# A newly laid order for the first eight pairs of an attention and feed-forward kernel, with third buffers and other load queues

## The chip, the cores and the metric

The kernel runs on one core of a Trainium2 chip. The metric is the device time of one execution in microseconds (us); smaller is better. The time before is 367.57 us, the median of 3 runs (366.59 to 367.79).

## The reference, cut to what matters

```python
q, k, v: (8, 8, 576, 64) float32; bias_table: (32, 8); w_in: (512, 2048); w_out: (2048, 512)

scores = q @ k.T / sqrt(64) + bias_table[bucket(|i - j|)]     # by batch and head
attn = softmax(scores)
x = (attn @ v) with batch and position as 4608 rows, heads side by side as 512 columns
h = x @ w_in
out = max(0.01 * h, h) @ w_out                                # (4608, 512) float32
```

The bias depends on the distance |i - j| alone, and from a distance of 128 on it is one constant for each head.

## The kernel before, in words

**Work items.** A pair is two heads of one batch; there are 32 pairs, four to a batch (`n_pairs` is 4), numbered 0 to 31. For each pair the kernel makes the transposed scores, the exponentials, the product with V and a division, and puts the result, transposed, into `xT`. Once the four pairs of a batch are in `xT`, the feed-forward of the finished tokens may run: blocks `T` of 512 tokens, each with 16 input pieces (four matmuls of 512 columns each, then the leaky relu into `gt`) and 16 output parts (four matmuls each; four parts make a 128-row slice of the output).

**A pair's steps, with their lines.** `load_qk` (L114) brings q and k with POOL's DMA queue, turned into bf16 on the way. `turned_pair` (L277 and L281) transposes them on TensorE into a bank of the pool `ps_m` (tag "m", two banks). `transpose_q` (L296) copies q to `qt`, `transpose_k` (L303) copies k to `kt`, and `apart` (L288) makes the two heads' last 64 keys stand apart. `qk_mm(n, u)` makes one of six groups of scores: u = 0 to 3 are 128 keys by 512 queries for both heads (L331, two matmuls on half of the rows each), u = 4 the last 64 queries (L324), u = 5 the last 64 keys (L334, L335). Groups 0 to 3 and 5 go to the pool `ps_s` (two buffers), group 4 goes to the two banks of `ps_o` (tags "o0" and "o1"). `exp(n, u)` is ScalarE's exponential into the pair's buffers `at` and `at4` (L344, L351, L355). `band(n, u)` (L371, VectorE) multiplies the part near the diagonal by the bias factors `hk`; groups 0, 1, 2, 4 and 5 have such a part. `av_tails` (L384) and `av` (L395) multiply by V into the banks "o0" and "o1", one for each head, and `divide` (L404, L406) normalizes into `opair`. `x_transposes` (L451, L452) turns that through a bank "m" and copies it into `xT`; for pairs 6 to 30, except 7, a DMA does it (L441).

**The bias factors.** The table is loaded on SP's queue (L155), turned by one exponential (L168), and spread over a row `ub` of 512 numbers for each head by copies (L171, L182, L185); of the eleven copies at L182 ScalarE has three and VectorE eight. The row is written to memory (`u_row`, L191) and read back on SP's queue as `hk` and `hk4` in seven loads (L193, L200): heads 0 and 1, then 2 and 3, then 4 to 7.

**The order.** Nothing is rescheduled: every engine runs its instructions in the order in which the program calls them, and each waits for what it needs. For pairs 0 to 4 the order is written out by hand with calls such as `score(n, u)`, which is `qk_mm` and `exp`. From pair 5 on a loop with a small planner (`plan`, `slot`, `moe_block`) places feed-forward pieces between the pairs' steps; from pair 8 on it uses bodies that run two products on the two halves of TensorE's rows (`body_in_halves` L639, `av_phase` L428, `body_in_lanes` L743). Until pair 8 it places 16 input pieces and 4 output parts. `spin` (L941) is TensorE work without use, which keeps its clock up.

**Buffers.** `qt`, `kt`, `at` and `at4` have two buffers each, pair n using number n % 2. `gt` has two buffers of 16 x 512.

**Loads.** POOL's queue issues them in program order: q and k of pair 0, of pairs 1 and 2, V of the first heads, and so on; at pair 0's `begin`, `load_w_in(0)` (half of `w_in`), V of batch 1 in four chunks, its tails, q and k of its heads 4 to 7, the second half of `w_in` and the first half of `w_out`; at pair 2 q and k of batch 2 and the second half of `w_out`.

Of the kernel before, what the change touches and what calls it, by code (L numbers as in the profile page):

```python
# [37 lines left out]
def kernel(  # L38
# [32 lines left out]
    qt_pool = ctx.enter_context(tc.tile_pool(name="qt", bufs=2))  # L71
# [10 lines left out]

    ident = per.tile([P, P], BF16, name="ident")
# [18 lines left out]
    own = per.tile([P, 2, SL], BF16, name="own")  # L102
    ATW = 2 * NJ * S
    at_ = [per.tile([P, ATW + SL], BF16, name=f"at{i}") for i in range(2)]
    at4_ = [per.tile([P, S + SL], BF16, name=f"at4_{i}") for i in range(2)]

# [42 lines left out]
    clear_edges(nc.vector, 0)  # L149
    nc.vector.memset(own, 0.0)  # L150
# [5 lines left out]
    load_qk(0, 0, 2)  # L156
# [16 lines left out]
    for u, lo, hi in bucket_runs(NB, BAND, S):  # L173
        if lo >= small:
            w = hi - lo + 1
            if groups and groups[-1][2] == w:
                groups[-1][3] += 1
            else:
                groups.append([u, lo, w, 1])
    for j, (u, lo, w, m) in enumerate(groups):  # L180
        copy = nc.scalar.copy if j % 3 == 2 else nc.vector.tensor_copy
        copy(out=ub[:, C0 + lo : C0 + lo + m * w].rearrange("h (m w) -> h m w", w=w),  # L182
             in_=e8[:, u : u + m].unsqueeze(2).to_broadcast([H, m, w]))
# [108 lines left out]

    def transpose_q(n):
        qt = qts[n] = qt_pool.tile([P, S], BF16, name="qt")
        copy = nc.scalar.copy if n <= n_pairs and n != 1 else nc.vector.tensor_copy
        copy(out=qt[:, 0:S].rearrange("p (r c) -> p r c", c=NC), in_=turned_pair(n, 0))  # L296

    def transpose_k(n):
        kt = kts[n] = kts_[n % 2]
# [10 lines left out]
    def qk_mm(n, u, swapped=False):  # L310

        qt, kt = qts[n], kts[n]
        if u == NJ:
            if in_lanes(n):
                t = ps_s_pool.tile([P, 2, 512], FP32, name="ps_s")
                ps = [t[:, e, :] for e in range(2)]
            elif swapped:
# [8 lines left out]
            return t if in_lanes(n) else ps  # L326
# [10 lines left out]

    def at_view(n):
        return at_[n % 2][:, 0:ATW].rearrange("p (e c i) -> p e c i", e=2, c=NJ)

    def exp(n, u, ps):
        at, at4 = at_view(n), at4_[n % 2]
        if u < NJ:
            nc.scalar.activation(at[:, :, u, 0:512], ps, AF.Exp, scale=scale)  # L344
        elif u == NJ and in_lanes(n):
# [8 lines left out]
        else:  # L354
            nc.scalar.activation(at4[:, 0:S], ps.rearrange("p e i -> p (e i)")[:, 0:S], AF.Exp, scale=scale)  # L355

    def band(n, u):
        b, p = items[n]
        at, at4 = at_view(n), at4_[n % 2]
# [5 lines left out]
        elif u == NJ:  # L365
            o, m = at[:, :, 3, 2 * P : S], mirrored(hp, 0, S - 2 * P)
        elif u == NJ + 1:
            o, m = at4[:, 3 * P : S], mirrored(hk4[:, p, :], 0, P + SL)
# [6 lines left out]
    def av_tails(n):  # L375

        b, p = items[n]
        at4 = at4_[n % 2]
        ops_[n] = op_pool.tile([P, NJ + 1, 2 * D], BF16, name="opair")
        ps = outs[n] = [ps_o_pool.tile([P, 512], FP32, name="ps_o", tag=f"o{e}") for e in range(2)]  # L380
        for ic in range(NJ + 1):
# [5 lines left out]

    def av(n, e):
        b, p = items[n]
        at = at_[n % 2]  # L390
        ps = outs[n][e][:, 0 : (NJ + 1) * (D + 1)].rearrange("p (i d) -> p i d", d=D + 1)
        for ic in range(NJ + 1):
            for c in range(NJ):
                o = (e * NJ + c) * S + ic * P
                nc.tensor.matmul(ps[:, ic, :], lhsT=at[:, o : o + P], rhs=vn[b % NBUF][:, c, 2 * p + e, :],  # L395
                                 start=False, stop=(ic == NJ and c == NJ - 1))
        divide(n, (e,))

    def divide(n, heads):
        opair = ops_[n]  # L400
        of = [outs[n][e][:, 0 : (NJ + 1) * (D + 1)].rearrange("p (i d) -> p i d", d=D + 1) for e in heads]
        rcps = [rc_pool.tile([P, NJ + 1, 1], FP32, name="rcp") for _ in heads]
        for ps, rcp in zip(of, rcps):
            nc.vector.reciprocal(rcp, ps[:, :, D : D + 1])  # L404
        for e, ps, rcp in zip(heads, of, rcps):
            nc.vector.tensor_tensor(out=opair[:, :, e * D : (e + 1) * D], in0=ps[:, :, 0:D],  # L406
                                    in1=rcp.to_broadcast([P, NJ + 1, D]), op=ALU.mult)
# [9 lines left out]
    def av_phase(n, phase, last=None):  # L417

        b, p = items[n]
        at = at_[n % 2]  # L420
# [14 lines left out]

    def x_transposes(n, spare=None):
# [13 lines left out]
        for ic in range(NJ + 1):  # L450
            nc.tensor.transpose(ps[:, ic * P : (ic + 1) * P], in_=opair[:, ic, :], identity=ident)  # L451
        nc.vector.tensor_copy(out=xT[p][:, b * S : (b + 1) * S], in_=ps[:, 0:S])  # L452

# [13 lines left out]

    def ffn_in(T, f, spare=None):
        if f == 0:
            gts[T] = gt_pool.tile([P, n_fc, TT], BF16, name="gt")  # L470
        t0 = T * TT
# [4 lines left out]
        for c in range(n_cc):  # L476
            nc.tensor.matmul(pm, lhsT=w_in_sb[:, c, f * P : (f + 1) * P], rhs=xT[c][:, t0 : t0 + TT],  # L477
                             start=(c == 0), stop=(c == n_cc - 1))
# [86 lines left out]
    def choose():  # L565
# [4 lines left out]
        return "in" if left("in") == 0 or left("in") * share >= left("out") * n_fc else "out"  # L570

# [408 lines left out]
    def spread_loads(n, part):  # L980
# [3 lines left out]
        nc.gpsimd.tensor_copy(out=tick, in_=at4_[n % 2][0:1, S - 1 : S] if part == 2 else  # L984
# [30 lines left out]
    spin(9)  # L1015
    transpose_q(0)
    transpose_k(0)
    spin(2)
    score(0, 0)
    score(0, 1)  # L1020
    begin(0)
    score(0, 2)
    score(0, 3)
    transpose_q(1)
    transpose_k(1)
    spin(2)
    score(0, 5)
    score(0, 4)
    transpose_k(2)
    score(1, 0)  # L1030
    score(1, 1)
    score(1, 4)

    begin(1)
    for u in (0, 1, 2, 5, 4):
        band(0, u)
    spin(3, ps_m_pool, "m")
    score(1, 2)
    spin(3, ps_m_pool, "m")
    score(1, 3)  # L1040
    transpose_q(2)
    band(1, 0)
    band(1, 1)
    av_tails(0)
    av(0, 0)
    score(1, 5)
    av(0, 1)
    score(2, 0)
    score(2, 1)
    x_transposes(0)  # L1050
    band(1, 2)

    begin(2)
    band(1, 5)
    band(1, 4)
    transpose_k(3)
    score(2, 2)
    score(2, 3)
    av_tails(1)
    av(1, 0)  # L1060
    band(2, 0)
    transpose_q(3)
    score(2, 5)
    av(1, 1)
    band(2, 1)
    score(3, 0)
    x_transposes(1)
    band(2, 2)
    score(2, 4)
    score(3, 1)  # L1070

    for n in range(3, n_pairs):
        begin(n)
        band(n - 1, 5)
        band(n - 1, 4)
        transpose_k(n + 1)
        score(n, 2)
        av_tails(n - 1)
        av(n - 1, 0)
        band(n, 0)  # L1080
        score(n, 3)
        av(n - 1, 1)
        transpose_q(n + 1)
        score(n, 5)
        band(n, 1)
        x_transposes(n - 1)
        band(n, 2)
        score(n, 4)
        score(n + 1, 0)
        score(n + 1, 1)  # L1090

    n = n_pairs
    begin(n)
    band(n - 1, 5)
    band(n - 1, 4)
    av_tails(n - 1)
    av(n - 1, 0)
    score(n, 2)
    av(n - 1, 1)
    score(n, 3)  # L1100
    transpose_k(n + 1)
    x_transposes(n - 1)
    finished(n - 1)
    band(n, 0)
    band(n, 1)
    score(n, 5)
    room["left"] = 4
    moe(1)
    band(n, 2)
    transpose_q(n + 1)  # L1110
    score(n, 4)
    moe(2)
    band(n, 5)
    band(n, 4)
    pair_rows(n + 2)
    moe(1)

    for n in range(n_pairs + 1, N + 1):
# [121 lines left out]
```

## Time and profile before

| what | value |
|---|---|
| median of 3 runs | 367.57 us |
| the profiled execution's own time | 366.07 us |
| its span, first to last instruction | 364.3 us |
| busy: TensorE, weight loads, VectorE, ScalarE, POOL | 355.5, 205.7, 190.6, 243.8, 98.3 us |
| granted TensorE clock, mean | 0.999 |
| HBM read and written | 37.68 and 9.45 MB |

Times in the profile count from the span's start. In a timeline row stand the start, the duration, the engine, the line, the operation, what is written and read, the count of merged instructions, and in brackets how long the engine had been idle before and what ended that. In the chain of waits each piece is what the end of the program hung on at that time. A busy TensorE is not TensorE at its peak, because matmuls overlap and their ends are modelled.

### The profile page before, as it was taken

The numbers are of one execution on the slowest core, as the hardware profiler recorded it, in microseconds if no ns is written. First come the engines' busy times: TensorE is split into PE (matmuls) and PEld (weight loads), VectorE is DVE, ScalarE is ACT, GpSimd is POOL, SyncE is SP. The second block draws the span as 40 slices with busy tenths as digits, with TensorE's granted clock in tenths as the row PEclk, the third lists the DMA queues.
The fourth block names the chain that finished last, engine by engine and source line by source line (L and its number), as shares of the span: only waits on it lengthen the run. The fifth ranks groups of instructions, "written<-read, shape, count | busy, mean of one in ns | idle before, by whom it ended". The sixth has DMA issues, their size and how long they took to land.

```text
span 364.3 us, 11901 instructions
## 1 busy us (share of the span) xinstructions
PE 355.5 (98%) x5081; PEld 205.7 (56%) x5101; DVE 190.6 (52%) x499; ACT 243.8 (67%) x364; POOL 98.3 (27%) x190
## 2 busy tenths in 40 slices
PE   7999999999999999999999999999999999999996
PEld 2565565555557776666666666656666544444443
DVE  3797887677755767555656665555554300200000
ACT  5998887479948888777777777777776274054111
POOL 8854422042334334423243334211000000000000
PEclk9999999999999999999999999999999999999999
DMA  8999999999898898998898989965113000200212
GB/s 100 196 196 175 207 205 140 154 166 112 99 138 128 104 155 126 140 130 125 119 126 127 115 123 129 122 107 98 49 50 49 31 29 0 88 29 0 86 60 86
DMA packets 104651, 40.26 MB, mean 111 GB/s; under 512 B 83472, under 2 KB 99096, under 8 KB 104600
## 3 DMA queue, kind: packets, MB, share of 16 engines
q0 software_dynamic: 53984, 18.36, 49.6%
q1 hardware_dynamic: 49320, 19.06, 27.1%
q10 hardware_dynamic: 1296, 2.10, 1.6%
q8 instruction: 40, 0.66, 0.8%
q14 instruction: 11, 0.09, 0.1%
HBM read 37.68 MB, written 9.45 MB: 129 GB/s over the span
## 4 chain that ended last, share of the span: by engine, by line
PE 90%; DMA 4%; DVE 2%; SPq 1%; ACT 1%; issue 1%; ACTq 0%; DVEq 0%
PE pm L743 35%; PE pm L477 16%; PE pm L518 16%; PE ps_o L428 7%; PE ps_s L331 7%; DMA hk<-u_row 3%; PE ps_o L395 3%; PE pm L639 1%; PE ps_o L384 1%; PE ps_s L743 1%; DMA u_row<-ub 1%; PE ps_tx L451 1%; PE pm L511 1%; SPq L200 1%; PE ps_s L324 1%
## 5 line engine op out<-in xcount | busy, mean ns | idle before, releaser
L344 ACT ACTIVATE at<-ps_s 128x1024 bf16<-128x1024 f32 x128 | 126.1, 1023 | 31.6 <-PE ps_s L331 31.6
L743 PE MATMUL pm<-xT,w_in_sb 64*128 64x512 bf16 x608 | 139.6, 376 | 0.0
L743 PE MATMUL pm<-w_out_sb,gt 64*128 64x512 bf16 x544 | 129.6, 376 | 0.0
L490 ACT ACTIVATE gt<-pm 128x512 bf16<-128x512 f32 x140 | 82.5, 602 | 41.9 <-PE pm L477 36.2
L371 DVE TENSOR_TENSOR at<-at,hk 128x768 bf16<-128x768 bf16 (+3 forms) x160 | 69.0, 451 | 31.4 <-ACT at L355 20.4
L743 PEld LDWEIGHTS <-w_in_sb 64*128 64x128 bf16 x608 | 51.8, 94 | 24.7 <-issue 1.2
L477 PE MATMUL pm<-xT,w_in_sb 128*128 128x512 bf16 x257 | 60.7, 379 | 0.7
L743 PEld LDWEIGHTS <-gt 64*128 64x128 bf16 x544 | 48.3, 94 | 22.1 <-issue 0.7
L518 PE MATMUL pm<-w_out_sb,gt 128*128 128x512 bf16 x260 | 58.9, 379 | 0.8 <-issue 0.5
L331 PE MATMUL ps_s<-qt,kt 64*128 64x512 bf16 x256 | 46.5, 378 | 1.7 <-ACT at L344 1.2
L518 PEld LDWEIGHTS <-gt 128*128 128x128 bf16 x268 | 25.6, 98 | 29.9
L477 PEld LDWEIGHTS <-w_in_sb 128*128 128x128 bf16 x268 | 25.2, 98 | 28.6
L121 POOL DMA_DIRECT2D vn<-in_v_dram x32 | 33.7, 1054 | 20.4 <-PE pm L743 5.2
L428 PEld LDWEIGHTS <-at 64*128 64x128 bf16 x1760 | 33.1, 94 | 3.8 <-issue 0.5
L428 PE MATMUL ps_o<-vn,at 64*128 64x65 bf16 x1760 | 35.2, 190 | 0.0
L355 ACT ACTIVATE at<-ps_s 128x576 bf16<-128x576 f32 x32 | 21.0, 657 | 18.4 <-PE pm L743 18.1
L984 POOL COPY tick<-opair 1x1 bf16<-1x1 bf16 x46 | 8.3, 181 | 81.9 <-DVE opair L406 81.6
L406 DVE TENSOR_TENSOR opair<-ps_o,rcp 128x320 bf16<-128x320 f32 x64 | 29.4, 488 | 1.5
L794 DVE COPY y<-pm 128x512 f32<-128x512 f32 x17 | 11.8, 692 | 27.6 <-PE pm L743 27.6
L531 DVE COPY y<-pm 128x512 f32<-128x512 f32 x11 | 7.6, 691 | 33.6 <-PE pm L518 30.8
L984 POOL COPY tick<-at 1x1 bf16<-1x1 bf16 x23 | 4.9, 213 | 62.3 <-DVE at L371 62.3
L331 PEld LDWEIGHTS <-kt 64*128 64x128 bf16 x256 | 13.7, 94 | 13.5 <-issue 6.6
(76 smaller groups left out, 321.9 us busy)
## 6 DMA issues: line engine op xcount, KB each, us to landing
out_dram<-y SPq DMA_DIRECT2D x28, 256.0 KB, 3.1
vn<-in_v_dram POOLq DMA_DIRECT2D x28, 128.0 KB, 4.5
qn<-in_q_dram POOLq DMA_DIRECT2D x22, 144.0 KB, 4.1
kn<-in_k_dram POOLq DMA_DIRECT2D x22, 144.0 KB, 3.3
w_in_sb<-in_moe_w_in_dram POOLq DMA_DIRECT2D x2, 1024.0 KB, 12.2
w_out_sb<-in_moe_w_out_dram POOLq DMA_DIRECT2D x2, 1024.0 KB, 17.4
out_dram<-y ACTq DMA_DIRECT2D x7, 256.0 KB, 2.0
qn<-in_q_dram POOLq DMA_DIRECT2D x5, 288.0 KB, 10.3
```

The lines of the kernel that those rows point to most:

```text
L121: nc.gpsimd.dma_start(out=vn[b % NBUF][:, c, h0:h1, 0:D], in_=v[b, h0:h1, c * P : (c + 1) * P, :].rearrange("h s d -> s h d"),)
L331: nc.tensor.matmul(ps[:, e, :], lhsT=kt[r, u * P : (u + 1) * P], rhs=qt[r, 0:512], start=True, stop=True)
L344: nc.scalar.activation(at[:, :, u, 0:512], ps, AF.Exp, scale=scale)
L355: nc.scalar.activation(at4[:, 0:S], ps.rearrange("p e i -> p (e i)")[:, 0:S], AF.Exp, scale=scale)
L371: nc.vector.tensor_tensor(out=o, in0=o, in1=m, op=ALU.mult)
L406: nc.vector.tensor_tensor(out=opair[:, :, e * D : (e + 1) * D], in0=ps[:, :, 0:D], in1=rcp.to_broadcast([P, NJ + 1, D]), op=ALU.mult)
L428: m = nc.tensor.matmul(outs[n][e][:, ic * (D + 1) : (ic + 1) * (D + 1)], lhsT=at[halves[r], o : o + P], rhs=vn[b % NBUF][halves[r], c, 2 * ...
L477: nc.tensor.matmul(pm, lhsT=w_in_sb[:, c, f * P : (f + 1) * P], rhs=xT[c][:, t0 : t0 + TT], start=(c == 0), stop=(c == n_cc - 1))
L490: nc.scalar.activation(g, pm, AF.Prelu, bias=0.0, scale=1.0, alpha=0.01)
L518: nc.tensor.matmul(pm, lhsT=gt[:, f, ts * P : (ts + 1) * P], rhs=w_out_sb[:, f, :], start=(f == 0), stop=(f == n_fc - 1))
L743: m = nc.tensor.matmul(o, lhsT=w, rhs=x, start=was is None, stop=need[bank] == 0)
L984: nc.gpsimd.tensor_copy(out=tick, in_=at4_[n % 2][0:1, S - 1 : S] if part == 2 else ops_[n - 2 + part][0:1, 0, 0:1])
```

## The change

1. The first pair's q is loaded as float32 on ScalarE's queue, as the program's first instruction, and ScalarE casts it into `qn`, after the exponential of the table. POOL's first load is k alone.
2. All eleven copies of the bias row are VectorE's.
3. `qt`, `kt`, `at` and `at4` get a third buffer, cut out of one of the two `gt` tiles, which isn't needed before block 1. Pairs 0 to 5 use number n % 3, later ones n % 2.
4. Pairs 0 to 7 run in an order that is a list of tokens, in place of the code by hand and of three turns of the loop. In it matmuls and exponentials, transposes and their copies, and the divisions are single steps; the product with V goes by chunks of 128 keys (`ac n e c`, all query blocks of a chunk); group 4's scores can take a `ps_s` buffer (`m n 4 s`, then one exponential for both heads); two input pieces of the feed-forward are begun on three of their four steps before pair 3 is there (`p0`, ended by `p1`); input pieces and their leaky relu are apart (`i`, `l`), with banks of `ps_m`, `ps_s` or `ps_o`. It holds the same 16 input pieces and 4 output parts. The q copies of pairs 5 and 7 move from VectorE to ScalarE.
5. `w_in` comes in quarters, V of batch 1 by single heads first, q and k of its heads 4 to 7 in two loads each.

The diff, cut to its core (`at_[n % 2]` becomes `at_[home(n)]` and likewise throughout; `blocks(n)` and `width(n)` are the old constants):

```diff
+    first_q = per.tile([96, 2, S // 96, D], FP32, name="first_q")
+    nc.scalar.dma_start(out=first_q.rearrange("r h c d -> r h (c d)"),
+                        in_=q[0, 0:2, :, :].rearrange("h (r c) d -> r h (c d)", c=S // 96))
...
+    early = gt_pool.tile([P, n_fc, TT], BF16, name="gt").rearrange("p f t -> p (f t)")
+    ATE = ATW + SL
+    at_.append(early[:, 0:ATE])
+    at4_.append(early[:, ATE : ATE + S + SL])
+    kts_.append(early[:, ATE + S + SL : ATE + 2 * S + SL + P])
+    qts_ = [per.tile([P, S], BF16, name=f"qt{i}") for i in range(2)]
+    qts_.append(early[:, ATE + 2 * S + SL + P : ATE + 3 * S + SL + P])
+
+    def home(n):
+        return n % 3 if n <= n_pairs + 1 else n % 2
...
+    clear_edges(nc.vector, 2)
...
-    load_qk(0, 0, 2)
+    load_qk(0, 0, 2, ("k",))
...
+    nc.scalar.copy(out=qn[0][0:RQ, 0:2, :, :], in_=first_q)
     for j, (u, lo, w, m) in enumerate(groups):
-        copy = nc.scalar.copy if j % 3 == 2 else nc.vector.tensor_copy
+        copy = nc.vector.tensor_copy
...
-    def load_w_in(half):
-        o = slice(half * (DF // 2), (half + 1) * (DF // 2))
+    def load_w_in(quarter):
+        o = slice(quarter * (DF // 4), (quarter + 1) * (DF // 4))
...
+    def av_chunks(n, e, chunks):
+
+        b, p = items[n]
+        at = at_[home(n)]
+        for c in chunks:
+            for ic in range(blocks(n)):
+                o = (e * NJ + c) * S + ic * P
+                nc.tensor.matmul(outs[n][e][:, ic * (D + 1) : (ic + 1) * (D + 1)], lhsT=at[:, o : o + P],
+                                 rhs=vn[b % NBUF][:, c, 2 * p + e, :],
+                                 start=False, stop=(ic == blocks(n) - 1 and c == NJ - 1))
...
+    def first_part():
+        T, f = step("in")
+        if f == 0:
+            gts[T] = gt_pool.tile([P, n_fc, TT], BF16, name="gt")
+        pm = bank("pm1")
+        in_steps(pm, T, f, range(n_cc - 1))
+        return pm, T, f
+
+    def last_part(pm, T, f, by_vector=0):
+        in_steps(pm, T, f, (n_cc - 1,))
+        leaky(T, f, pm, by_vector)
+        room["left"] -= 1
...
         if n == 0:
             load_w_in(0)
-            load_v_part(1, range(NJ))
+            load_w_in(1)
+            load_v_head(1, 0)
+            load_v_head(1, 1)
             load_v_tail(1)
-            load_qk(1, H // 2, H)
-            load_w_in(1)
+            load_qk(1, 4, 6)
+            load_v_head(1, 2)
+            load_v_head(1, 3)
+            load_w_in(2)
+            load_qk(1, 6, H)
+            load_w_in(3)
+            load_v_part(1, range(NJ), 4, H)
             load_w_out(0)
...
+    first = """
+        spin 9 o, tq 0, tk 0, cq 0 a, ck 0, ap 0, m 0 0, spin 2 o, e 0 0,
+        begin 0, m 0 1, tq 1, e 0 1, m 0 2, e 0 2, tk 1, m 0 5, ck 1, e 0 5, cq 1 v, spin 2 o, m 0 4,
+        m 0 3, e 0 4, ap 1, e 0 3, tk 2, m 1 0, ck 2, spin 3 m, tq 2, b 0 4, e 1 0, m 1 1, b 0 5, b 0 0,
+        b 0 1, e 1 1,
+        begin 1, m 1 4 s, e 1 4, spin 3 m, m 1 2, b 0 2, m 1 3, at 0, ac 0 1 0, ac 0 0 0, ac 0 1 1, b 1 0,
+        b 1 1, cq 2 a, ac 0 1 2, ap 2, e 1 2, ac 0 0 1, e 1 3, ac 0 0 2, m 1 5, e 1 5, ac 0 0 3, dv 0 0,
+        m 2 0, ac 0 1 3, m 2 1, dv 0 1, e 2 0, b 1 5, tk 3, ck 3, m 2 3, e 2 1, tq 3, b 1 2, ap 3, at 1,
+        b 1 4, m 2 2,
+        begin 2, e 2 3, ac 1 0 0, ac 1 0 1, ac 1 0 2, ac 1 1 0, b 2 0, cq 3 a, ac 1 0 3, ac 1 1 1,
+        ac 1 1 2, xt 0, e 2 2, m 2 5, e 2 5, ac 1 1 3, dv 1 0, dv 1 1, m 3 0, m 2 4, xc 0, b 2 5, e 3 0,
+        b 2 1, b 2 2, tk 4, m 3 2, e 2 4, m 3 1, at 2, b 2 4, ac 2 0 0, xt 1,
+        begin 3, ac 2 1 0, e 3 2, e 3 1, ck 4, m 3 3, xc 1, ac 2 0 1, ap 4, ac 2 0 2, b 3 0, ac 2 0 3,
+        dv 2 0, ac 2 1 1, tq 4, ac 2 1 2, e 3 3, ac 2 1 3, m 3 5, m 3 4 s, cq 4 a, e 3 5, tq 5, dv 2 1,
+        m 4 0, xt 2, e 3 4, b 3 1, e 4 0, m 4 1, e 4 1, b 3 5, b 3 2,
+        begin 4, b 3 4, at 3, ac 3 0 0, ac 3 1 0, ac 3 0 1, ac 3 1 1, b 4 0, ac 3 1 2, ac 3 1 3, ac 3 0 2,
+        ac 3 0 3, fin 3, m 4 3, xc 2, cq 5 a, m 4 2, dv 3 0.1, p0 0, xt 3 o0, b 4 1, e 4 2, p0 1, xc 3,
+        e 4 3, p1 0 0, p1 1 0, m 4 5, m 4 4 s, tk 5, rows 6, e 4 4, ck 5, e 4 5, ap 5, moe, b 4 5, b 4 2,
+        moe, tq 6, b 4 4, m 5 0, m 5 1, at 4, cq 6 v,
+        begin 5, ac 4 1 0, ac 4 0 0, ac 4 1 1, ac 4 0 1, e 5 0, ac 4 0 2, ac 4 0 3, ac 4 1 2, b 5 0, m 5 5,
+        dv 4 0, ac 4 1 3, tk 6, e 5 1, e 5 5, dv 4 1, i m, m 5 2, m 5 3, m 5 4, ck 6, b 5 1, xt 4, rows 7,
+        l 0, b 5 5, e 5 3, e 5 2, e 5 4, i m, xc 4, i s, l 1, ap 6, l 0, i s, i m, at 5, l 0,
...
```

The list goes on in the same manner through pairs 6 and 7, and the loop begins at pair 8. In the list `tq`, `tk`, `cq`, `ck`, `ap` are the transposes, copies and `apart`; `m`, `e`, `b` scores, exponentials and bands; `at`, `ac`, `dv` tails, chunks and division; `xt`, `xc` the way into `xT`; `a` and `v` name ScalarE and VectorE.

More of the change, by code (lines that the diff above doesn't have):

```diff
@@ L475, in ffn_in @@
             pm = ps_o_pool.tile([P, 512], FP32, name="pm1", tag=f"o{spare}")
-        for c in range(n_cc):
-            nc.tensor.matmul(pm, lhsT=w_in_sb[:, c, f * P : (f + 1) * P], rhs=xT[c][:, t0 : t0 + TT],
-                             start=(c == 0), stop=(c == n_cc - 1))
+        in_steps(pm, T, f, range(n_cc))
         return pm
@@ L1013, in score @@
         exp(n, u, qk_mm(n, u))
[L1015 to L1090, printed above, removed]
@@ L1119 @@
+    tps, held_, open_ = {}, {}, []
+    for t in first.replace("\n", " ").split(","):
+        if t.strip():
+            tok([word(w) for w in t.split()])
+    for n in range(2 * n_pairs, N + 1):
         live = n < N
```

169 lines of the change are left out of this document (111 added, 58 removed).

## The prediction

> **What bounds the kernel now.** I read the page first, then the table by stretches, the chain of waits, and the timeline of the first 63 us.
>
> ```profile
> span 364.3 us, 11901 instructions
> PE 355.5 (98%) x5081; PEld 205.7 (56%) x5101; DVE 190.6 (52%) x499; ACT 243.8 (67%) x364; POOL 98.3 (27%) x190
> ```
>
> TensorE is busy for 98% of the span, so a gain can only come from a stretch in which it has too little to do. The table by stretches shows which that is (busy us of PE, PEld, DVE, ACT, POOL, each with its count):
>
> ```profile
> 5.00:10.00 5.00, 3.59 (x57) 1.78 (x55) 1.47 (x4) 3.86 (x5) 4.99 (x8) 1.00 1.29 150
> 12.94:21.30 8.36, 7.73 (x154) 5.03 (x152) 7.04 (x20) 8.36 (x12) 5.29 (x10) 1.00 1.35 204
> 21.30:29.04 7.74, 6.95 (x143) 4.44 (x140) 7.44 (x20) 7.58 (x13) 4.19 (x6) 1.00 1.57 192
> 32.85:62.21 29.36, 29.03 (x344) 16.24 (x346) 23.31 (x56) 23.42 (x38) 10.25 (x16) 1.00 1.62 187
> ```
>
> Three stages. Up to 12.94 the pipeline fills. From 12.94 to about 29 ScalarE and VectorE are both full (8.36 of 8.36 and 7.58 of 7.74 us; 7.04 and 7.44 us): they set the pace while the first batch's four pairs go through, because the feed-forward can't begin before all four are done. From 32.85 to 62.21, where pair 8 starts, TensorE is busy 29.03 of 29.36 us. The chain of waits says the same:
>
> ```profile
> 4.58 3.45 DMA u_row<-ub
> 11.67 9.53 DMA hk<-u_row
> 21.30 0.42 DVE at L371
> 31.51 0.45 PE ps_tx L451 x5
> 43.34 1.73 PE pm L477 x8
> 46.72 0.61 PE ps_o L395 x20
> 62.29 0.32 PE ps_s L331 x2
> ```
>
> It runs through the bias row written to memory, the last of the loads that read it back (`hk`, heads 4 to 7, landed at 21.2), the first band of pair 2, and pair 3's way into `xT`; from there it is TensorE alone. So in the first 30 us the chain does not pass through the first q load at all.
>
> **The plan of the sum.** Both orders finish the same work before pair 8: 16 input pieces and 4 output parts (listed: 2 split, 2 planned and 12 single input pieces, 4 outputs). Everything from pair 8 on is unchanged and TensorE-bound, so the change is worth what it moves pair 8's first scores, now at 62.21. That time is the moment T when pair 3 is in `xT` (now 32.82, the end of the copy below), plus the TensorE work left then.
>
> **The start.**
>
> ```profile
> 4.70 0.50 PEld L281 LDWEIGHTS <-qn 96*64 96x64 bf16 x12 [0.84 <-DMA qn<-in_q_dram]
> 5.40 0.34 PEld L281 LDWEIGHTS <-kn 96*64 96x64 bf16 x12 [0.19 <-DMA kn<-in_k_dram]
> 5.44 0.64 ACT L296 COPY qt<-ps_t 128x576 bf16<-128x576 bf16 x1 [1.54 <-PE ps_t L281]
> 6.78 3.77 ACT L344 ACTIVATE at<-ps_s 128x1024 bf16<-128x1024 f32 x4 [0.70 <-PE ps_s L331]
> 361.64 0.34 ACTq L515 DMA_DIRECT2D out_dram<-y  x1
> 3.59 0.67 DVE L182 COPY ub<-e 8x12 bf16<-8x12 bf16 x8
> 4.37 0.18 DVE L185 COPY ub<-ub 8x127 bf16<-8x127 bf16 x1
> 12.94 1.96 DVE L371 TENSOR_TENSOR at<-at,hk 128x512 bf16<-128x512 bf16 x5 [0.49 <-DMA hk<-u_row]
> ```
>
> q's issue on ScalarE costs 0.34 us ahead of the table load, and ScalarE later has 1.54 us idle, which covers it and the added cast (96x768: between 0.64 us for 576 columns and 3.77/4 = 0.94 for 1024, so 0.8). k becomes POOL's first load and should land when q does now, 4.70 instead of 5.40. Everything up to the first exp moves by the same 0.7, with ends of 0 (q lands late) and 0.9: first exp at about 6.1. But this does not reach T. The bands wait for `hk`, and its source row comes later: three more copies of 0.67/8 = 0.08 us each go to VectorE, less the 0.1 us that VectorE now stands before L185, so the row leaves 0.15 us later and the first band starts at about 13.1. Two more edge fills stand where VectorE waits for the table: nothing. So the gain on ScalarE is slack, and VectorE's queue decides.
>
> **VectorE from the bands to T.** The rows that carry it:
>
> ```profile
> 18.03 0.46 DVE L452 COPY xT<-ps_tx 128x576 bf16<-128x576 bf16 x1 [0.69 <-PE ps_tx L451]
> 20.38 0.20 DVE L404 RECIPROCAL rcp<-ps_o 128x5 f32<-128x5 f32 x1
> 20.61 0.49 DVE L406 TENSOR_TENSOR opair<-ps_o,rcp 128x320 bf16<-128x320 f32 x1
> 21.30 0.42 DVE L371 TENSOR_TENSOR at<-at,hk 128x512 bf16<-128x512 bf16 x1 [0.20 <-DMA hk<-u_row]
> 27.92 1.12 DVE L371 TENSOR_TENSOR at<-at,hk 128x768 bf16<-128x768 bf16 x3
> 30.74 0.20 DVE L404 RECIPROCAL rcp<-ps_o 128x5 f32<-128x5 f32 x1 [0.34 <-PE ps_o L395]
> 32.37 0.45 DVE L452 COPY xT<-ps_tx 128x576 bf16<-128x576 bf16 x1
> ```
>
> Now VectorE reaches pair 2's first band 0.20 us before its `hk` lands, having done pair 0's x copy (0.46) and pair 1's first division (0.20+0.49) in the meantime. The new order puts both, and the second division, behind that band (`b 2 0` before `dv 1 0`, `dv 1 1`, `xc 0`). VectorE therefore gets there some 1.2 us earlier, about 20.0, and stands. A wait is added and behind it queue the divisions that free both output banks, so `m 2 4`, which writes those banks, and its exp are late too (a hole of some 0.5 us on ScalarE, paid by the 0.7 won at the start). From the landing, VectorE has 7.44 us of work to pair 3's last band now; the new order adds 0.64 and 0.40 (the two above, less 0.05 of overlap each when back to back) and puts pair 2's x copy (0.42) off past it: 8.06, and 0.1 for joints. With `hk` at 21.3: 29.46 instead of 29.04.
>
> Behind it the new order is shorter. Half of pair 3's attention-times-V runs before the last bands, so its end comes about 0.6 us after them instead of 1.70 (30.74 less 29.04): 30.1. Both divisions together (1.2, begun at 30.45 behind pair 4's first band and pair 2's copy), transposes and x copy follow, and no k copy stands before the copy as now: T = 32.70 against 32.82. With `hk` landing by 20.0 T would be 1.3 less.
>
> Where does `hk` land? It was issued at 11.67 and took 9.53 us.
>
> ```profile
> DMA to landing us min/median/max: 4.8/5.2/6.7
> 11.19 0.64 POOL L114 DMA_DIRECT2D kn<-in_k_dram  x1 [0.37 <-DMA kn<-in_k_dram]
> 18.18 0.31 PEld L281 LDWEIGHTS <-kn 96*64 96x64 bf16 x12 [0.36 <-DMA kn<-in_k_dram]
> ```
>
> The loads of its kind whose landing that view gives, all smaller, took 6.7 us at most (this one would have been there by 18.4), so the ends are 18.4 and, with the later row and a busier start, 21.9. POOL's loads now run 0.65 us ahead and one of them is off its queue; I take 20.9, near the load's own row, which moves T to 32.3. The Trainium skill, page "DMA: Bandwidth & Descriptors", section on queues, rings and completion order, says that each DMA engine takes turns between the queues that have work, a packet at a time. By that rule emptying POOL's queue by one load doesn't help SP's `hk` at all, and T would be 32.85 (an estimate from that page's rule). The trace agrees so far: POOL's k load issued at 11.19 landed at 18.2, before an SP load issued 0.5 us later that took 9.5.
>
> **TensorE from T to pair 8.**
>
> ```profile
> 32.24 1.02 PE L477 MATMUL pm<-xT,w_in_sb 128*128 128x512 bf16 x3
> 33.19 0.45 PE L281 MATMUL ps_t<-ident,qn 96*64 96x96 bf16 x12
> 28.86 0.78 PE L395 MATMUL ps_o<-vn,at 128*128 128x65 bf16 x20
> 29.57 0.39 PE L331 MATMUL ps_s<-qt,kt 64*128 64x512 bf16 x2
> 29.90 0.79 PE L395 MATMUL ps_o<-vn,at 128*128 128x65 bf16 x20
> ```
>
> Now 29.36 us are left. Of the input pieces three of four steps wait ready at T; the new order has six steps done on two pieces (1.73/8 = 0.216 each, so 0.65 more), and pair 5's q transposes (0.38). It has not done pair 4's tail scores (0.44, from a pair of matmuls at 31.80 to 32.24) nor pair 5's k transposes (0.38). Left: 29.36 - 0.65 - 0.38 + 0.44 + 0.38 = 29.15. Two additions. Scores on half the rows set between full-row matmuls cost more than their 0.216: 29.90 less 29.57 is 0.33, so 0.12 extra, up to 0.22 with the slow exit before it (29.57 less 28.86 is 0.71, where the chain has 0.61 for 20). I count two more such places after T: +0.3. And ScalarE is now behind at T, with exps of pair 4 and the first leaky ones queued, while both `m` banks hold split pieces, so pair 5's transposes wait: 0.1 to 0.4, I take 0.1 beyond what the 29.36 holds. Sum: 32.3 + 29.15 + 0.3 + 0.1 = 61.85, a gain of 0.4.
>
> **Edits at nothing.**
>
> ```profile
> 29.23 0.67 POOL L114 DMA_DIRECT2D kn<-in_k_dram  x1 [2.60 <-DMA w_in_sb<-in_moe_w_in_dram]
> 55.42 0.61 POOL L134 DMA_DIRECT2D v<-in_v_dram  x1 [4.51 <-DMA w_out_sb<-in_moe_w_out_dram]
> 58.43 1.89 PE L518 MATMUL pm<-w_out_sb,gt 128*128 128x512 bf16 x7
> ```
>
> w_in's first half is there at 29.2 and first used at 32.24, the last of w_out at 55.4 and used after 58.43: 3 us of cover each. The eight further issues on POOL (0.65 to 0.9 us) fall where it waits for landings. If they delay the loads by more than 3 us, each further us is lost. The third buffers free ScalarE from waiting on finished pairs, but it had no such wait to lose in its full stretch.
>
> **How it sums.** The profiled execution took 366.07 us for its 364.3 of span; the median of the runs is 367.57. A gain of 0.4 on the span gives 363.9, 365.7 for such an execution, and 367.2 against the median. A measurement of this kernel can tell about 0.3%, 1.1 us, from no change, so my forecast is: no change that can be told. Its own range is 366.5 to 368.6, from `hk` at 20.4 with no added wait behind T to `hk` at 22.0 with 0.3 more.
>
> **Rivals.**
> - Faster: `hk`'s last load lands before VectorE gets there (the others took at most 6.7 us). Then T is 31.4 and pair 8 starts at 60.95, 1.3 us sooner, or 1.7 without the 0.4 added behind T: 366.1 as its middle. At best the start's 0.7 to 0.9 come on top, if the first bands follow it: 364.9. For it: 1.3 us of VectorE waiting are all that holds the new order. Against: the load's own 9.53 us. Chance 0.36.
> - Slower: VectorE held at `b 2 0`. Nothing stands on its queue ahead of that band any more to use the wait, so every us of later landing moves T by one: `hk` at 21.3 breaks even (32.70 + 29.55 = 62.25), from 22.4 on it loses over 1.1 us, and at 23.0 the time is 369.3. For it: the row leaves later, and the load shares the engines with POOL's. Against: 0.15 us of delay is far from 1.1. With 0.5 us of further waits for banks behind T the point comes down to 21.9. Chance 0.20.
> - The change doesn't do what it says, q lands no sooner than now: the start's 0.7 us are lost, ScalarE's hole is then uncovered, and T moves by 0.5 at most: 367.6. It lies within my forecast, and so does `hk` landing at 21.45, as late as its row leaves it (T 32.85, pair 8 at 62.4, 367.8; the skill's rule above would give this one): 0.1 for each, and 0.44 for the forecast with both.
>
> **How the numbers follow.** The range reaches from the fast rival's best, 364.9, to the slow one's 369.3 and leaves out about a tenth on each side. The chances are those of the three cases, the last bullet's two counted with the forecast.
>
> **What would show it.** First exp near 6.1 rather than 6.78; a wait of VectorE for `hk` of over 1 us before pair 2's first band (right) or none (the fast rival); first `pm` closed at about 32.5; pair 8's first scores at 61.85. I am wrong if pair 8 starts before 61.0 or after 63.2, or if the time from T to pair 8 leaves 29 to 30 us.

## The result

| | before | after |
|---|---|---|
| median of 20 runs each | 367.56 us (366.31 to 369.77) | 370.71 us (367.90 to 374.88) |
| ratio | | 1.0078, 95% interval 1.0056 to 1.0099 |
| the profiled execution, its span | 366.07, 364.3 us | 371.99, 370.0 us |
| granted TensorE clock, mean | 0.999 | 0.985 |

The changed kernel is slower by 0.8%, above the range that was forecast. (The ratio leaves out its slowest execution, 374.88 us, which counts as a slow run.) The two profiled executions differ by more than the medians do: that of the kernel before lies 1.5 us under its median, that of the changed kernel 1.3 us over it. The shares below are those of these two executions. The changed kernel's chain of waits begins like that of the kernel before and is late from its first piece on (start, length, what the end of the program hung on):

```profile
0.74 3.66 DMA tabT<-in_bias_table_dram
6.19 3.70 DMA u_row<-ub
10.93 9.10 DMA hk<-u_row
20.13 1.07 DVE at L405 x3
21.25 1.61 PE ps_o L429 x26
68.04 0.32 PE ps_s L358 x2
```

Pair 8's first scores are at 68.04 where the kernel before has them at 62.29: 5.75 us later, and the span is 5.7 us longer. So in these executions all of it is lost ahead of pair 8, and nothing is lost or won behind it. The timeline of the changed kernel shows where (start, duration, engine, line, operation, and in brackets the idle time before it with its releaser):

```profile
0.73 0.39 ACTq L83 DMA_DIRECT2D first_q<-in_q_dram  x1
0.74 0.40 SPq L169 DMA_DIRECT2D tabT<-in_bias_table_dram  x1
4.43 0.14 DVE L181 TENSOR_SCALAR negc<-tabT 8x1 f32<-8x1 f32 x1 [2.05 <-DMA tabT<-in_bias_table_dram]
4.83 0.81 ACT L194 CAST qn<-first_q 96x768 bf16<-96x768 f32 x1
5.70 0.45 PE L296 MATMUL ps_t<-ident,qn 96*64 96x96 bf16 x12 [1.32 <-ACT qn L194]
6.19 0.28 SPq L206 DMA_DIRECT2D u_row<-ub  x1
7.30 1.02 ACT L377 ACTIVATE at<-ps_s 128x1024 bf16<-128x1024 f32 x1 [0.48 <-PE ps_s L358]
9.91 0.41 SPq L208 DMA_DIRECT2D hk<-u_row  x1
16.52 0.49 DVE L405 TENSOR_TENSOR at<-at,hk 128x640 bf16<-128x640 bf16 x1 [3.37 <-DMA hk<-u_row]
20.13 2.34 DVE L405 TENSOR_TENSOR at<-at,hk 128x192 bf16<-128x192 bf16 x6 [3.12 <-DMA hk<-u_row]
20.44 0.29 PE L418 MATMUL ps_o<-v,at 64*128 64x65 bf16 x4 [4.23 <-DVE at L405]
```

The same steps in the kernel before (the first row uses the table, the second writes the bias row, the third begins to read it back):

```profile
2.98 0.14 DVE L167 TENSOR_SCALAR negc<-tabT 8x1 f32<-8x1 f32 x1 [0.75 <-DMA tabT<-in_bias_table_dram]
4.58 0.28 SPq L191 DMA_DIRECT2D u_row<-ub  x1
8.05 0.41 SPq L193 DMA_DIRECT2D hk<-u_row  x1
```

The reader is to see three things. The table of 256 numbers, issued at the same moment as in the kernel before, is used at 4.43 instead of 2.98, the row leaves at 6.19 instead of 4.58, and its read-backs start at 9.91 instead of 8.05. The first band waits 3.37 us for the first read-back and starts at 16.52 instead of 12.94. The next, `b 0 5`, waits 3.12 us more, for a load of `hk4` issued at 10.93, and starts at 20.13; the list has it ahead of `b 0 0` and `b 0 1`, and TensorE's tails of pair 0 wait 4.23 us for it. And q itself, for whose sake part 1 was there, is no sooner in TensorE: its transposes start at 5.70, against 4.70, and the first exponential at 7.30, against 6.78.

What TensorE loses by this stands in the table by stretches of the changed kernel (stretch, length, busy us of PE, PEld, DVE, ACT and POOL with their counts, then granted clock, DMA share, GB/s):

```profile
5.00:10.00 5.00, 3.83 (x48) 1.73 (x50) 2.32 (x18) 3.36 (x5) 5.00 (x9) 0.72 1.52 155
10.00:15.00 5.00, 4.64 (x66) 2.33 (x66) 2.31 (x4) 4.88 (x7) 5.00 (x11) 0.93 1.06 110
15.00:20.00 5.00, 1.17 (x11) 0.36 (x10) 0.49 (x1) 3.05 (x5) 1.54 (x4) 0.75 1.24 203
20.00:25.00 5.00, 4.45 (x62) 3.05 (x62) 3.59 (x11) 1.46 (x2) 2.16 (x4) 0.57 1.56 208
```

and in the kernel before:

```profile
10.00:15.00 5.00, 4.85 (x71) 2.30 (x71) 4.17 (x10) 4.93 (x9) 4.46 (x7) 1.00 1.38 180
15.00:20.00 5.00, 4.37 (x92) 3.01 (x91) 4.05 (x11) 5.00 (x8) 2.88 (x6) 1.00 1.25 221
20.00:25.00 5.00, 4.51 (x107) 3.21 (x103) 4.62 (x13) 4.84 (x9) 2.91 (x4) 1.00 1.56 194
```

From 15 to 20 us TensorE has 1.17 us of work instead of 4.37. From 20 to 25 us it looks as busy as before (4.45 against 4.51), but it has 62 matmuls instead of 107 (not the same mix of sizes): its granted clock is 0.57 there. A busy share beside a low clock isn't work done. Not every execution of the changed kernel has this drop: of the 19 that count in the ratio, the four with a mean clock of 1.00 took 368.7 us on average, the four with 0.994 or 0.995 took 369.6, and the eleven with 0.985 to 0.991 took 371.2.

### The profile page after: what moved, and what is told of

It is laid out like the page before. It is cut to its first block, busy times and chain, and to the rows that moved or that the text cites. A ratio compares the mean times of both kernels' runs of the same rounds, so it can differ in the third digit from the quotient of the medians.

```text
span 370.0 us, 11893 instructions
## 1 busy us (share of the span) xinstructions
PE 357.2 (97%) x5080; PEld 211.8 (57%) x5101; DVE 189.0 (51%) x502; ACT 244.9 (66%) x361; POOL 103.2 (28%) x197
## 4 chain that ended last, share of the span: by engine, by line
PE 91%; DMA 4%; ACT 2%; DVE 1%; issue 1%; SPq 0%; ACTq 0%; DVEq 0%
PE pm L817 34%; PE pm L529 16%; PE pm L579 16%; PE ps_s L358 7%; PE ps_o L473 7%; DMA hk<-u_row 2%; PE ps_o L429 2%; PE pm L713 1%; PE ps_o L418 1%; PE ps_o L439 1%; PE ps_s L817 1%; DMA u_row<-ub 1%; DMA tabT<-in_bias_table_dram 1%; PE pm L572 1%; PE ps_s L361 1%; PE ps_s L351 1%
## 5 line engine op out<-in xcount | busy, mean ns | idle before, releaser
L377 ACT ACTIVATE at<-ps_s 128x1024 bf16<-128x1024 f32 x120 | 118.7, 1023 | 33.4 <-PE ps_s L358 32.8
L405 DVE TENSOR_TENSOR at<-at,hk 128x768 bf16<-128x768 bf16 (+3 forms) x150 | 65.1, 451 | 38.1 <-ACT at L389 20.5
L358 PE MATMUL ps_s<-qt,kt 64*128 64x512 bf16 x240 | 45.1, 382 | 0.8 <-ACT qt L311 0.5
L389 ACT ACTIVATE at<-ps_s 128x576 bf16<-128x576 f32 x30 | 19.7, 657 | 23.4 <-PE pm L817 18.1
L127 POOL DMA_DIRECT2D kn<-in_k_dram x28 | 18.4, 656 | 9.0 <-issue 5.9
## 6 DMA issues: line engine op xcount, KB each, us to landing
w_out_sb<-in_moe_w_out_dram POOLq DMA_DIRECT2D x2, 1024.0 KB, 13.1
```

Source lines behind the costliest of these rows:

```text
L127: nc.gpsimd.dma_start(out=dst[0:RQ, h0:h1, :, :].rearrange("r h c d -> r h (c d)"), in_=src[b, h0:h1, :, :].rearrange("h (r c) d -> r h (c ...
L358: nc.tensor.matmul(ps[:, e, :], lhsT=kt[r, u * P : (u + 1) * P], rhs=qt[r, 0:512], start=True, stop=True)
L389: nc.scalar.activation(at4[:, 0:w], ps.rearrange("p e i -> p (e i)")[:, 0:w], AF.Exp, scale=scale)
L405: nc.vector.tensor_tensor(out=o, in0=o, in1=m, op=ALU.mult)
```

## The experiments

The theories at the start. **A**: q's load on ScalarE's queue, at the same moment as the table's, holds up the table, and with it the row, its read-backs and the first bands. **B**: the new order by itself loses (part 4). **C**: the new loads (part 5) crowd out the read-backs. In each run the ratio is to the kernel before on the same chip, with its 95% interval.

**Part 1 alone.** The kernel before with q on ScalarE's queue and nothing else of the change.

```diff
+    nc.scalar.dma_start(out=first_q..., in_=q[0, 0:2, :, :]...)
...
-    load_qk(0, 0, 2)
+    load_qk(0, 0, 2, ("k",))
...
+    nc.scalar.copy(out=qn[0][0:RQ, 0:2, :, :], in_=first_q)
```

> The kernel before with one part alone: the first pair's q as float32 on ScalarE's queue, cast by ScalarE, k first on POOL's. Theory A: the table is used at about 4.4 us instead of 2.98, the row leaves about 1.5 later than at 4.58, the first band is 1.5 to 3.5 us later than 12.94, and the time is 1 to 3 us longer, 368.5 to 370.5. Theory B: within 0.6 us of 367.6, with the first exp earlier than 6.78.

Measured: 371.97 us, ratio 1.0132 (1.0109 to 1.0155). Its timeline, the table's use:

```profile
4.44 0.14 DVE L170 TENSOR_SCALAR negc<-tabT 8x1 f32<-8x1 f32 x1 [2.20 <-DMA tabT<-in_bias_table_dram]
```

The table is as late as in the whole change (4.43), with the old order and the old loads. Pair 8 starts at 68.92, 6.6 us later than in the kernel before, the span is 6.6 us longer, and the chain runs through the table, the row and `hk`. The time is above the 368.5 to 370.5 expected: one part of five loses more by itself than all five together. A is borne out. Here TensorE was slow in another way too. The same twelve transposes take 0.69 us until 13.84 and 0.45 from 17.85 on, where the kernel before has them at 0.45 from 9.09 on; the profile gives a clock of 1.00 throughout. That stretch isn't on the chain, and what it costs was not measured.

**All but part 1.** The changed kernel with its first q back on POOL's queue.

> The changed kernel with the first pair's q on POOL's queue again, ahead of k, and without ScalarE's cast; all else as changed. Theory A (q's packets on ScalarE's queue hold up the 256-number table, so the bias row, hk and the first bands are late): the table is used at about 3.0 us instead of 4.43, the row leaves at about 4.7 instead of 6.19, the first band starts before 14 instead of at 16.5, and the time falls by 2 to 4 us, to 366.5 to 368.5. Theory B (the new order itself costs the time, whatever the table does): it stays at 369.5 to 371.5.

Measured: 367.90 us, ratio 1.0029 (1.0007 to 1.0051). Most of the loss is gone, and the profile shows the case that the prediction had worked out. Pieces of its chain of waits (start, length):

```profile
2.95 0.15 DVE negc L178
4.80 3.22 DMA u_row<-ub
11.65 9.62 DMA hk<-u_row
21.36 0.42 DVE gt L401
61.71 0.32 PE ps_s L354 x2
63.00 13.82 DMA tu<-pr
```

The table is used where it was in the kernel before (2.95 against 2.98), and the row leaves 0.22 us later than there. Pair 8 comes at 61.71, 0.58 us sooner than in the kernel before. But then the chain leaves TensorE again, for the transposes by DMA of the next pairs (`tu`), 13.82 us. The waits from 60 to 85 us name who stood for them (waiter, releaser, us in all, times, longest):

```profile
DVE qt L319 <- DMA tu<-pr: 6.4, 2, 4.8
PE ps_o L414 <- DVE xT L508: 1.9, 1, 1.9
```

From pair 8 to the end this execution took 3.5 us more than the kernel before. That is a second loss, and the whole change doesn't show it: there pair 8 comes 5.7 us later, and the transposes by DMA take 4.7 us from issue to landing (median of three) instead of 12.0.

**q behind the table in one queue.** The changed kernel with the same q load moved from ScalarE's queue to SP's, behind the table's.

```diff
-    nc.scalar.dma_start(out=first_q..., in_=q[0, 0:2, :, :]...)
...
     nc.sync.dma_start(out=tabT, in_=bias_table.rearrange("u h -> h u"))
+    nc.sync.dma_start(out=first_q..., in_=q[0, 0:2, :, :]...)
```

> The changed kernel with the first q's float32 load issued on SP's queue right behind the table, in place of ScalarE's queue. Theory A: the table's 256 packets go ahead of q's on the same queue, it is used at about 3.0 us, and the time is 366.5 to 368.5, with q some 0.4 us later than in the changed kernel. Theory B, and a form of A in which any second load beside the table delays it: no gain, 369.5 to 371.5.

Measured: 367.79 us, ratio 1.0023 (1.0003 to 1.0043). Its timeline:

```profile
3.11 0.14 DVE L181 TENSOR_SCALAR negc<-tabT 8x1 f32<-8x1 f32 x1 [0.73 <-DMA tabT<-in_bias_table_dram]
4.36 0.83 ACT L194 CAST qn<-first_q 96x768 bf16<-96x768 f32 x1 [0.75 <-DMA first_q<-in_q_dram]
```

The same bytes in the same stretch, one behind the other: the table is there at 3.11, and q is cast from 4.36 on, sooner than its cast began (4.83) when both ran side by side and the cast stood behind the late table.

**Half the dose.** The kernel before with one head of q on ScalarE's queue and the other on POOL's.

```diff
-    first_q = per.tile([96, 2, S // 96, D], FP32, name="first_q")
+    first_q = per.tile([96, 1, S // 96, D], FP32, name="first_q")
...
+    load_qk(0, 1, 2, ("q",))
     load_qk(0, 0, 2, ("k",))
```

> The kernel before with half of the first pair's q (one head, 144 KB read) by ScalarE's queue as float32 and the other half by POOL's queue as before. Theory A (the table's small packets take turns with q's packets on the same DMA engines, so the delay goes by the number of q's packets): `negc` half-way between 2.98 and 4.44, at 3.6 to 3.8, and the row's write half-way, at 5.3 to 5.5. Rival (a fixed delay, by two queues starting at the same moment, whatever their size): `negc` at 4.4 and the row at 6.2, as with the whole q. Rival (it is the bytes that fill the engines only at the end of q's transfer, so that a transfer that is over sooner does not meet the table): `negc` at 3.0. The time: by the row's delay between 367 and 371; first exp later than in the kernel before, since the second half of q is cast in POOL's queue behind the small set-up.

Measured: 368.19 us, ratio 1.0037 (1.0017 to 1.0057). Its timeline:

```profile
3.55 0.14 DVE L171 TENSOR_SCALAR negc<-tabT 8x1 f32<-8x1 f32 x1 [1.32 <-DMA tabT<-in_bias_table_dram]
5.34 0.28 SPq L196 DMA_DIRECT2D u_row<-ub  x1
```

The table is just ahead of the 3.6 to 3.8 expected for half the packets, and the row within its 5.3 to 5.5. The DMA queues in the first 6 us (packets, MB, share of the 16 engines) of the run with half of q:

```profile
q10 hardware_dynamic: 112, 0.15, 9.0%
```

and of the changed kernel, where the second row is SP's queue with the table:

```profile
q10 hardware_dynamic: 208, 0.29, 16.0%
q1 hardware_dynamic: 264, 0.00, 2.5%
```

With none, 112 and 208 packets on the other queue the table is used at 2.98, 3.55 and 4.43. The delay grows with the packets (0.57 and 1.45 us, somewhat more than in proportion), so the fixed delay of the one rival and the free passage of the other are both out. These are single executions, but the table's use moves little between them: 2.89 to 2.98 in the nine profiled kernels with no such load beside it, 4.43 and 4.44 in the three with the whole of q. SP's 264 packets hold next to no bytes, so it isn't their own bytes that take the time; that they wait for q's packets at the same engines is the reading that fits, and no view shows it packet by packet. Whether each of them waits its turn, or all of an engine's together for q's share of it, these runs don't tell apart.

**The other parts.** The changed kernel with the old loads (part 5 undone), then the new order with neither part 1 nor part 5 (parts 2 and 3 are in it), then part 5 alone on the kernel before.

> The changed kernel with batch 1's loads and w_in as before: w_in in halves, V of batch 1 in four chunks, the old order. Theory A: no effect on the first bands (w_in is issued after hk), 370 to 371.5. Rival C (w_in's quarters and the reordered loads crowd hk out, whose late part landed at 20 us): hk's loads land 2 to 4 us sooner and the time falls to 367 to 368.5.

> The changed kernel with the first q back on POOL and w_in and batch 1's loads as before, so that the new order, the third buffers and the bias row's copies are left. In the run with q back on POOL alone, pair 8's V product began at 62.02 (before: 62.60), but 3.5 us were lost behind it, where a DMA transpose of pairs 10's rows took 13.8 us to land. Theory A2 (w_in's quarters and the smaller loads put POOL's backlog 2 to 4 us later, and the transposes by DMA wait behind it): here the backlog ends as before, the transposes land as before, and the time is 366.3 to 367.2, at or below the kernel before. Theory B2 (reaching pair 8 earlier is itself what runs into the DMA backlog, or the order is slower elsewhere): the same 0.5 to 1.5 us above the kernel before.

> The kernel before with w_in in quarters and batch 1's loads in the new sequence, nothing else. Theory A2: POOL's backlog ends 2 to 4 us later, pair 9's and 10's transposes by DMA land later than pair 8 and 9 need them, and the time is 0.5 to 2.5 us longer. Theory B2: within 0.4 us of the kernel before, since w_in and V are there in time in both.

Measured: 371.79 us, 1.0114 (1.0084 to 1.0144); 370.20, 1.0079 (1.0052 to 1.0107); 368.01, 1.0036 (1.0020 to 1.0053). C falls as the main cause: without the new loads the change is no faster. The second result went against the expectation: the new order is worse with the old loads (1.0079) than with the new ones (1.0029), though the new loads by themselves cost 0.36%. Parts 4 and 5 are no sum; the order needs something of the loads. The new loads' own cost has the same face as behind pair 8 above; chain and waits of the last run:

```profile
58.62 13.09 DMA tu<-pr
```

```profile
DVE qt L296 <- DMA tu<-pr: 4.7, 1, 4.7
PE ps_o L384 <- DVE xT L452: 1.8, 1, 1.8
```

The kernel before waits 2.4 us there and TensorE not at all. The bytes are the same, the cuts and their sequence are not. But old loads don't spare a kernel this wait: in one below (`rows 6` moved, old loads) it is 4.3 us.

**What the order needs.** The profiled execution of the run with the new order alone, its fastest, showed no large wait. The next kernel, which also moves `b 2 0` behind both divisions and pair 0's x copy (the wait on which the prediction hung), showed it.

```diff
-  ... ac 1 1 0, b 2 0, cq 3 a, ... dv 1 0, dv 1 1, m 3 0, m 2 4, xc 0, b 2 5,
+  ... ac 1 1 0, cq 3 a, ... dv 1 0, dv 1 1, m 3 0, m 2 4, xc 0, b 2 0, b 2 5,
```

> As the run with the new order alone, with one token moved: pair 2's first band behind pair 1's two divisions and pair 0's x copy on VectorE's queue, as in the kernel before. The prediction's step (VectorE stands some 1.2 us at that band for the last hk load, with this work queued behind it): the wait of 0.99 us seen there falls to under 0.3, pair 3 is in xT 0.5 to 1.0 us earlier, pair 8 starts about 61.3, and the time is 0.4 to 1.0 us below the run with the new order alone, unless the transposes by DMA take it back behind pair 8. Rival: the wait is hidden by ScalarE's exps, no change.

Measured: 370.18 us, ratio 1.0090 (1.0060 to 1.0119). The gain of 0.4 to 1.0 us didn't come; the wait of 0.99 us that was to go had been seen with q back on POOL's queue, and the profiled execution of the new order alone doesn't have it. The waits from 30 to 50 us:

```profile
DVE pr L270 <- DMA qn<-in_q_dram: 4.3, 1, 4.3
PE pm L525 <- DVE gt L313: 3.8, 1, 3.8
```

VectorE stands 4.3 us in `rows 6` for q of the second sequence's heads 4 and 5, which the old loads bring at 37.2. Behind it in its queue stands `ck 5`, the copy of pair 5's k that frees a bank, and for that bank TensorE stands 3.8 us. So in the next kernel, otherwise the same, `rows 6` was moved behind it:

```diff
-  m 4 4 s, tk 5, rows 6, e 4 4, ck 5, e 4 5, ap 5, moe, b 4 5, b 4 2, moe, tq 6,
+  m 4 4 s, tk 5, e 4 4, ck 5, e 4 5, ap 5, moe, b 4 5, b 4 2, moe, rows 6, tq 6,
```

> The new order with the old start and the old loads, the band `b 2 0` behind the divisions, and the step `rows 6` moved four steps of VectorE's order back, from ahead of `ck 5` to just ahead of `tq 6`. Theory A3 (the step `rows 6` waits on VectorE for heads 4 and 5 of the second sequence, which the old loads bring at 37.2 us, and with 4.30 us of that wait holds up `ck 5`, the band products of pair 4 and so TensorE): the gap of 3.80 us at 39.32 and the half clock at 38.91 are gone, pair 8 starts at 62 to 64 instead of 67.36, and the time falls by 2 to 4 us, to 366 to 368. Rival B (the new order is slower by itself behind pair 3, whatever this wait): pair 8 stays at 66 or later, the time at 370.

Measured: 367.13 us, ratio 1.0016 (0.9997 to 1.0035), where it was 1.0090 without the move. Its timeline:

```profile
36.08 0.36 DVE L270 COPY pr<-qn 96x768 bf16<-96x768 bf16 x1 [0.21 <-DMA qn<-in_q_dram]
```

The wait for q is 0.21 us (q is there 1.1 us sooner too), and with it most of the loss is gone.

**One transfer moved.** If that is all that the order needs, the old loads do with one change: q and k of heads 4 to 7 ahead of V, nothing cut. First in the new order, then with `b 2 0` moved as well, then in the kernel before.

```diff
             load_w_in(0)
+            load_qk(1, H // 2, H)
             load_v_part(1, range(NJ))
             load_v_tail(1)
-            load_qk(1, H // 2, H)
             load_w_in(1)
```

> The new order with the old start, w_in in halves, and the old loads with one transfer moved: q and k of heads 4 to 7 of the second sequence are issued ahead of its V instead of behind it; no transfer is cut or added. Theory A3 (what the new order needs of the new loads is only that q and k come sooner, and what the new loads cost is that w_in in quarters and V in pieces make the backlog of POOL's queue end later): no wait for qn at `rows 6`, pair 8 at 62 to 62.6, the rest behind it 301.6 to 302, so 365.5 to 366.7, ratio 0.997 to 1.000. Rival B (the order itself loses): 368 or more. Rival D (the backlog comes from moving q and k ahead at all): pair 8 at 62, but 3 us lost behind it at the transposes by DMA, as in the run with q back on POOL.

> The same as the run before, and `b 2 0` behind the two divisions and the copy of xT. Theory of the prediction (VectorE's wait of 1 us at that step sets when pair 3 is in xT): T comes 0.5 to 1 us sooner than 32.91, pair 8 at 61 to 62, 0.5 us less in the time. Rival E (the wait lies beside TensorE's work, which is what T follows): T at 32.9, pair 8 the same as without the move, no difference that 5 rounds tell.

> The kernel before with the same one transfer moved (q and k of heads 4 to 7 ahead of V of the second sequence), nothing else. If the move by itself is free or a gain: 366 to 367, ratio 0.998 to 1.001, no matter for the old order, whose rows of pair 6 stand later. Rival D (the move makes V's backlog late): the wait for the transposes by DMA behind pair 8 grows beyond 2.4 us and the time by 1 to 2 us.

Measured: 366.79 us, 0.9995 (0.9978 to 1.0012); 365.91, 0.9967 (0.9949 to 0.9984); 366.61, 0.9993 (0.9977 to 1.0010). With q on POOL's queue and one transfer moved the new order is level with the kernel before. For the transposes by DMA VectorE waits 0.4 us in the first of the three, 1.7 in the second and not at all in the third. With `b 2 0` moved the new order is the one version that beats both kernels, by 0.33% of the kernel before. The last copy of pair 3 into `xT` in the first of them

```profile
32.96 0.46 DVE L489 COPY xT<-ps_tx 128x576 bf16<-128x576 bf16 x1
```

and in the second:

```profile
31.76 0.46 DVE L489 COPY xT<-ps_tx 128x576 bf16<-128x576 bf16 x1
```

That is 1.2 us sooner, so between these two the wait at `b 2 0` does set T. Yet in the two profiled executions pair 8's products with V come at 62.69 and 62.84, no sooner. The second shows where the 1.2 us went:

```profile
37.54 0.46 PE L414 MATMUL ps_o<-v,at 64*128 64x65 bf16 x10 [1.04 <-DMA v<-in_v_dram]
```

TensorE reaches pair 4's tails 1.2 us sooner and stands there 1.04 us for a load of V, which the move has put behind q and k. So this order has a second need of the loads. What the 0.88 us between the two medians come from, the profiles don't show, and the two intervals overlap.

## Why the prediction was wrong

**The start, the step that failed.** The prediction had "the row leaves 0.15 us later", from three copies that go to VectorE, and priced q's issue on ScalarE as an instruction of 0.34 us covered by idle time. It priced the instruction (it took 0.39 us) and put at nothing what the transfer does to the table beside it. The row left 1.61 us later (6.19 against 4.58), 1.45 of it the table's delay; the 0.16 left is what the forecast had for the copies. The first exponential, forecast at 6.1, came at 7.30: q's cast stands in ScalarE's order behind the exponential of the same late table. That the change doesn't do what it says was a rival, but for a price of 0.5 us; this much of it was true, and the price was not.

The prediction had the rule that bears on this and used it at the wrong place. The Trainium skill, page "DMA: Bandwidth & Descriptors", section on queues, rings and completion order, says that each DMA engine takes turns between the queues with work, a packet at a time. The prediction weighed it for `hk` at 21 us. The runs with no, half and the whole of q agree with it for the table at 0.74: 2.98, 3.55, 4.43.

**From the row to the first bands.** Forecast 13.1, measured 16.52. The read-backs were issued 1.86 us later, so 1.7 us more come from slower landings: the row's write took 3.70 us until the first read-back against 3.45, and the first read-back 16.52 less 9.91, 6.6 us, against 4.9. Over the read-backs whose landing the view gives, the median is 8.9 us against 5.2. Part 1 alone shows such slower landings too (median 7.9), so the new loads aren't needed for it. That they meet more of POOL's transfers there is argued, not shown.

**VectorE held for `hk`, the slow rival.** Right in kind, and wrong in place, price and cause. It was laid at pair 2's first band, `b 2 0`, from 22.4 on, and went up to 369.3 us. It came at pair 0's bands, 6.5 us in two waits, where these executions lost 5.7 us. There the prediction saw VectorE's queue only; but TensorE has nothing else ready so early (1.17 of 5 us busy), and on top the clock went down.

**`b 2 0`, T and TensorE's rest: right in kind, once part 1 is undone, and partly by luck in the number.** With q back on POOL's queue the added wait is 0.99 us (forecast over 1), `hk` lands at 21.3 (20.9 taken), T is 32.91 (32.70 was worked out for a landing at 21.3, 32.3 for 20.9), and pair 8 starts at 61.71 against a forecast of 61.85. From T to pair 8 it is 28.80 us, in this run and in the changed kernel (39.24 to 68.04): below the 29 to 30 that the prediction allowed, and 0.75 under its 29.55; the two additions of 0.4 for short scores and a late ScalarE aren't seen in it. So pair 8 came near its forecast because T was 0.6 us late and the rest 0.75 us short. In the changed kernel itself T is 6.4 us later than in the kernel before (39.24 against 32.82), so its whole loss lies ahead of T.

**Behind pair 8 nothing changes: right for the changed kernel, wrong as a reason.** There it holds within 0.1 us (5.75 later at pair 8, 5.7 at the end). With part 1 undone 3.5 us are lost behind pair 8, where the chain runs 13.82 us through the transposes by DMA.

**Edits at nothing.** The loads were given 3 us of cover, read at the uses of `w_in` and `w_out`. They cost 0.36% by themselves, and the wait stands at a use that wasn't asked for: the transposes by DMA on SP's queue, which run beside the end of POOL's transfers. That the wait comes from the cuts alone is not shown, since the new order waits 4.3 us there with the old loads too. The third buffers and the bias row's copies were not tried by themselves.

So of the 0.78% that the change loses, 0.49 goes when part 1 is undone, and the 0.29 left are about what the new loads cost by themselves (0.36; each is known to some 0.2). The order of part 4 is level with the old one where its needs are met, and a little better with `b 2 0` moved.

## What to carry to other kernels

A load that is moved to an idle queue is not free because its engine is idle: look at what else is in flight at that moment, above all a small load of tiny packets at the head of the chain, and put the large one behind it in the same queue. A new order carries needs of its own on loads; find them from the in-order engine that waits first, and move the one transfer, rather than cut all of them. And follow a late start through to the end of the chain before calling it slack, since TensorE can pay twice, in idle time and then in its clock.

## What the runs showed of the hardware

- A table of 1 KB was 1.45 us late beside a load of 288 KB that was issued at the same moment on another queue, and 0.13 us late with the same load behind it on its own queue (3.11 against 2.98).
- TensorE stayed slow after a time without work. In the changed kernel the mean clock was 0.75 from 15 to 20 us, when it had 1.17 us of work, and 0.57 from 20 to 25 us, when it had work again. Twelve transposes that take 0.45 us at 5.70 take 0.69 at 8.70, where the clock is 0.50 (8 to 10 us):

```profile
8.70 0.69 PE L296 MATMUL ps_t<-ident,qn 96*64 96x96 bf16 x12
```

- At the start of these programs the profile's clock doesn't tell TensorE's speed. It reads 1.00, and yet the first twelve transposes of the kernel before take 0.69 us at 4.71 and later ones 0.45; with part 1 alone 0.69 lasts until 13.84.
- The transposes by DMA at 57 to 79 us had a median of 8.6 us from issue to landing in the kernel before (four of them), 12.0 with the new loads in the new order and q on POOL's queue (three), 8.7 with the new loads alone (three), 9.0 with the old loads in the new order (`rows 6` moved, four), and 5.5 with uncut loads and q and k first in the new order (four).
